# A fused beacon-attention and maxout-FFN kernel: the opening of batch 0 in another order, with fewer filler matmuls

## The chip, the cores and the metric

The kernel runs on one core of one Trainium2 chip. The metric is the device time of one execution in microseconds (us). A core has a matrix engine (TensorE, "PE" in the profile), a vector engine (VectorE, "DVE"), an activation engine (ScalarE, "ACT"), a general engine (GpSimd, "POOL") and an engine that only issues transfers (SyncE, "SP"). Each engine works through its own instructions in the order in which the program emits them, and waits at the head of its queue. Transfers between main memory (DRAM) and the on-chip memory run on sixteen shared DMA engines.

## What is computed

The reference, cut to what matters (B = 8 batches, H = 8 heads, S = 576 tokens, Nb = 16 beacons, D = 64; d_model = 512, d_ff = 768; inputs and output in float32):

```python
k_all = concatenate([beacon_k, k], axis=2)          # 16 + 576 keys
v_all = concatenate([beacon_v, v], axis=2)
scores = matmul(q, k_all.transpose(0, 1, 3, 2)) / sqrt(D)
scores = where(causal, -1e9, scores)                # beacons are seen by all
a = softmax(scores)
x = matmul(a, v_all).transpose(0, 2, 1, 3).reshape(B * S, H * D)
h = maximum(maximum(x @ w1, x @ w2), x @ w3)
out = h @ w_out                                     # 4608 x 512
```

## The kernel before, in words

**Work of attention.** Heads are taken two at a time: a *pair* is two heads of one batch, four pairs to a batch (`PPB`), 32 in all; pair p is heads 2(p mod 4) and 2(p mod 4)+1 of batch p div 4. Queries and keys of a pair arrive as rows of tokens, in bf16 or cast to it, and are turned by TensorE transposes against an identity (`turn_part` at line 331, `turn_cast` at 363, `turn_wide` at 380) or by DMA. VectorE and ScalarE copy the turned tiles from the accumulators (PSUM) into `qkT` (lines 338, 369, 387). `qkT` has room for four pairs. `turn_beacons` (line 299) and `place_beacons` (line 394) put the beacon keys ahead of the others.

Scores are computed transposed, keys by queries, in *windows* of at most 512 columns: `emit_window` gives a window's matmuls for both heads (line 476) and two exponentials on ScalarE that write the weights `at` in bf16 (line 485). `emit_mask` clears the upper triangle of a diagonal block: on GpSimd with a select (line 505), or on VectorE as a product with a 0/1 triangle `tri` (line 503). `emit_pv` multiplies weights by v with a column of ones behind it (line 529); VectorE takes the reciprocal of that column (line 539) and the product (line 541), which gives normalised rows of x. `turn_x` transposes them on TensorE (line 555) and copies them into `xT` (line 560); from batch 2 on a DMA does that.

**Work of the FFN.** The FFN is a list of *units* which `F(n)` emits in order. One unit of the first layer is a block of 128 hidden features for 512 tokens and one of the three weights (`mm1_unit`, line 592). For the first 240 tokens (`PART`), two blocks of features go together (`mm1_two`, line 606), three units for w1 and three for w2; these need only the first 240 tokens of all four pairs of batch 0. The units after them need 512 tokens. `F` emits nothing while the tokens that it needs aren't there (`avail`). VectorE drains a unit (a cast for w1 at line 582, a running maximum for w2 and w3 at line 584). Units of the second layer are `mm2_unit` (line 622), drained at line 630.

**Order of the work.** Everything is emitted in an order written out by hand. `opening()` (line 718) does batch 0 and the first window of batch 1; `loop()` (line 895) does the rest in *bursts* of three windows, and each burst emits FFN units until a goal for it is reached (`START`: 17 units by the end of burst 0, 20 by the end of burst 1).

In `opening()` the short names are: `T0(p, part)` turns part 0 (240 tokens) or 1 (336 tokens) of a pair, `W0(pi, i)` emits a window of pair pi (i = 0 is the first 240 queries; i = 2, 3, 4 are the query tiles behind them), `M0(pi, tiles, False)` masks on GpSimd and `M0(pi, tiles)` on VectorE, `P0` is the product with v, `X0` the turn of x. `idle(n)` (line 406) and `keep_busy(n)` (line 399) are matmuls of 128 and 320 columns on a tile of ones, into a bank whose content nobody reads.

**Loads of the opening.** Pairs 0 and 1 send their first part over SP and ACT as float32 (`load_part`, lines 161 and 168). The first part of pairs 2 and 3 (`load_quad(1, 0, i)`), the second part of pairs 0 and 1 (`load_quad(0, 1, i)`) and of pairs 2 and 3 (`load_quad(1, 1, i)`) are cast on the way by transfers from GpSimd's queue (line 176). So are v of batches 0 to 2 (`load_v`, line 233), the FFN weights (`load_w(i, f0, f1)` at line 282 for w1, w2, w3 as i = 0, 1, 2, each in two pieces of 512 and 256 features; `load_w_out` at line 286) and pairs 4 to 9 (`load_cast`, line 218; four buffers in turn). The beacon keys go over SP, eight small transfers (`load_beacons`, line 290). GpSimd spends time to issue each of its transfers, and its masks stand in the same queue. Later pairs come as float32 over SP (`load_wide`, line 198) and are cast by GpSimd (line 206); the first of them is held back by a memset on GpSimd. In `loop()`, `jobs` holds these loads with the burst in which each is issued.

Of the kernel before, what the change touches and what calls it, by code (L numbers as in the profile page):

```python
# [16 lines left out]
def kernel(  # L17
# [13 lines left out]
    nc = tc.nc  # L31
# [675 lines left out]
    def T0(p, part, q_copy=by_dve, k_copy=by_dve):  # L707
        turn_part(p, part, q_copy, k_copy)

    def P0(pi, *tiles):  # L710
        emit_pv(0, pi, tiles)
# [6 lines left out]
    def opening():  # L718
        keep_busy(12)
        load_part(0, 0, nc.sync)  # L720
        load_part(0, 1, nc.scalar)
        load_part(1, 0, nc.sync)
        load_part(1, 1, nc.scalar)
        load_beacons(0, 1, bk32_0)
# [15 lines left out]
        load_v(0, 0, 1)  # L740
        for i in range(2):
            load_quad(1, 1, i)
        load_w(0, 0, FA)
        cast_part(0, 0, by_dve)
        cast_part(0, 1, by_act)
        cast_part(1, 0, by_dve)
        cast_part(1, 1, by_dve)
        by_act(bk16_0, bk32_0)
        T0(0, 0, by_act)
        keep_busy(3)  # L750
        T0(1, 0)
        turn_beacons(0, 1, bk16_0)
        keep_busy(2)
        W0(0, 0)
        M0(0, (0, 1), False)
        idle(6)
        W0(1, 0)
        load_w(0, FA, d_ff)
        T0(2, 0)
        idle(6)  # L760
        T0(3, 0)
        W0(2, 0)
        idle(6)
        M0(1, (0, 1), False)
        load_v(0, 2, 3, 4)
        W0(3, 0)
        idle(6)
        M0(2, (0, 1), False)
        T0(0, 1)
        idle(6)  # L770
        W0(0, 2)
        M0(3, (0, 1))
        load_w(1, 0, FA)
        T0(1, 1)
        W0(0, 3)
        P0(0, 0, 1)
        idle(6)
        W0(0, 4)
        M0(0, (2, 3), False)
        P0(1, 0, 1)  # L780
        idle(6)
        W0(1, 2)
        load_w(1, FA, d_ff)
        X0(0, 0, 1)
        P0(2, 0, 1)
        idle(6)
        W0(1, 3)
        M0(0, (4,), False)
        T0(2, 1)
        X0(1, 0, 1)  # L790
        W0(1, 4)
        M0(1, (2, 3), False)
        P0(3, 0, 1)
        X0(2, 0, 1)
        idle(6)
        T0(3, 1)
        W0(2, 2)
        X0(3, 0, 1)
        F(1)
        load_beacons(1, B, bk32_1)  # L800
        W0(2, 3)
        M0(1, (4,), False)
        load_cast(4)
        F(1)
        W0(2, 4)
        load_cast(5)
        W0(3, 2)
        M0(2, (2, 3), False)
        F(1)
        W0(3, 3)  # L810
        M0(2, (4,), False)
        load_w(2, 0, FA)
        P0(0, 2, 3)
        P0(0, 4)
        W0(3, 4)
        load_w(2, FA, d_ff)
        M0(3, (2, 3), False)
        M0(3, (4,), False)
        X0(0, 2, 3, 4)
        P0(1, 2, 3)  # L820
        P0(1, 4)
        by_act(bk16_1, bk32_1)
        load_cast(6)
        load_v(1, 0, 1, 2, 3, 4)
        P0(2, 2, 3)
        F(1)
        X0(1, 2, 3, 4)
        turn_beacons(1, B, bk16_1)
        P0(2, 4)
        F(2)  # L830
        load_cast(7)
        turn_cast(4, by_act, by_dve)
        place_beacons(4, by_act)
        X0(2, 2, 3, 4)
        P0(3, 2, 3)
        P0(3, 4)
        emit_window(*ahead)
        X0(3, 2, 3, 4)
        F(2)
# [15 lines left out]
    jobs = []  # L855
    jobs.append((0, None, L(load_w_out, 0, n_ft // 2)))
    jobs.append((0, None, L(load_cast, 8)))
    jobs.append((0, None, L(load_v, 2, 0, 1)))
    jobs.append((1, None, L(load_w_out, n_ft // 2, n_ft)))
    jobs.append((1, None, L(load_v, 2, 2, 3, 4)))  # L860
    jobs.append((1, None, L(load_cast, 9)))
    jobs.append((1, None, L(next_load, 2)))
    for p in range(BY_CAST, NPAIR):
        if p in BY_DMA:
            jobs.append((first_burst[p] - 5, L(load_pair, p), L(cast_pair, p, by_pool)))
        else:
            gate = nc.gpsimd if p == BY_CAST else None
            c = first_burst[p] - 3
            jobs.append((c, L(load_wide, p, gate), L(cast_wide, p, by_pool)))
# [25 lines left out]
    def loop():  # L895
# [8 lines left out]
        for c, burst in enumerate(bursts):  # L904
# [10 lines left out]
            for p in range(PPB + 1, NPAIR):  # L915
                if first_burst[p] - 1 == c:
                    place_beacons(p, by_act)
                    if p < BY_CAST:
                        turn_cast(p, by_act, by_dve)
                    elif p not in BY_DMA:  # L920
                        turn_wide(p, by_act, by_dve)
# [99 lines left out]
```

## Time and profile before

| | |
|---|---|
| median of three runs | 283.21 us (283.15 to 283.51) |
| the profiled execution | 283.48 us |
| its span, first to last instruction | 281.8 us |
| TensorE busy | 275.3 us |
| GpSimd busy | 130.4 us |
| first transposes on TensorE | at 4.84 us |
| first FFN unit | at 18.65 us |
| first window of burst 1 | at 38.82 us |

Times inside the execution are counted from the start of the span. The profile names an instruction by its line in the kernel, its engine, what it writes and what it reads. A busy share says how long an engine had an instruction under way, not whether that instruction was of use; a row of the timeline gives start, length and count, and in brackets how long the engine had stood idle and what released it. The chain that ended last follows the work back from the last instruction, at each step to what released it.

### The profile page before, as it was taken

What the parts mean: (1) busy time and instruction counts of PE and PEld (TensorE: products, weight loads), DVE (VectorE), ACT (ScalarE), POOL (GpSimd) and SP (SyncE); (2) the same over time, 40 slices, a digit from 0 to 9 for tenths busy, and PEclk for the clock granted to TensorE, in tenths of its full rate; (3) what the DMA queues carried; (4) which work ended last, traced back from release to release, by engine and by line L of the source; (5) the groups of instructions that cost most, each with busy time, mean ns of one, the idle gap of its engine ahead of it and who ended that gap; (6) DMA issues with size and microseconds to landing.
All of it is one profiled execution on the core that took longest, in us unless ns stands there. A gap on an engine that the chain in (4) does not pass through costs nothing.

```text
span 281.8 us, 8016 instructions
## 1 busy us (share of the span) xinstructions
PE 275.3 (98%) x3121; PEld 158.3 (56%) x3121; DVE 198.6 (70%) x397; ACT 125.2 (44%) x274; POOL 130.4 (46%) x253
## 2 busy tenths in 40 slices
PE   7999999999999999999999999999999999999995
PEld 4678665666555555455555888555545554444442
DVE  4677776768777577667685777577757885876873
ACT  3677458887555454535553555444544100000000
POOL 8998789297664456446643645345422100000000
PEclk9999999999999999999999999999999999999999
DMA  8999999998993899999996999595342016003003
GB/s 143 187 187 197 174 131 138 238 301 194 228 190 79 264 242 217 174 295 214 237 245 182 256 221 165 157 276 134 76 130 77 0 37 198 0 0 151 0 0 150
DMA packets 87382, 45.68 MB, mean 162 GB/s; under 512 B 68400, under 2 KB 78512, under 8 KB 87344
## 3 DMA queue, kind: packets, MB, share of 16 engines
q1 hardware_dynamic: 63504, 37.25, 57.4%
q0 software_dynamic: 23488, 7.67, 25.3%
q8 instruction: 24, 0.39, 0.6%
q10 hardware_dynamic: 352, 0.25, 0.3%
q14 instruction: 14, 0.11, 0.2%
HBM read 35.13 MB, written 11.80 MB: 167 GB/s over the span
## 4 chain that ended last, share of the span: by engine, by line
PE 95%; DVE 2%; ACT 1%; issue 1%; ACTq 0%
PE ps L592 48%; PE ps L622 16%; PE ps L529 11%; PE ps L476 10%; PE ps L380 2%; PE ps L606 2%; PE ps L399 2%; PE ps L331 1%; PE ps L406 1%; PE ps L555 1%; ACT at L485 1%; PE ps L363 1%; DVE qkT L338 1%; PE ps L641 0%; DVE xT L560 0%
## 5 line engine op out<-in xcount | busy, mean ns | idle before, releaser
L592 PE MATMUL ps<-xT,w_sb 128*128 128x512 bf16 (+2 forms) x720 | 147.3, 351 | 0.1
L485 ACT ACTIVATE at<-ps 128x512 bf16<-128x512 f32 (+3 forms) x214 | 106.5, 601 | 87.8 <-PE ps L476 60.2
L592 PEld LDWEIGHTS <-w_sb 128*128 128x128 bf16 x720 | 65.4, 98 | 56.5 <-issue 4.1
L505 POOL TENSOR_SCALAR_AFFINE_SELECT at<-at 128x256 bf16<-128x256 bf16 (+2 forms) x158 | 57.3, 389 | 80.9 <-ACT at L485 71.1
L584 DVE TENSOR_TENSOR hT<-hT,ps 128x512 bf16<-128x512 bf16 (+2 forms) x111 | 74.6, 672 | 27.3 <-PE ps L592 26.2
L582 DVE CAST hT<-ps 128x512 bf16<-128x512 f32 (+2 forms) x57 | 37.7, 662 | 16.0 <-PE ps L592 13.2
L622 PE MATMUL ps<-w_out_sb,hT 128*128 128x512 bf16 x210 | 48.5, 379 | 0.0
L630 DVE COPY y<-ps 128x512 f32<-128x512 f32 x35 | 24.2, 692 | 25.2 <-PE ps L622 25.2
L529 PEld LDWEIGHTS <-at 128*128 128x128 bf16 (+1 forms) x960 | 35.5, 97 | 8.0
L529 PE MATMUL ps<-v,at 128*128 128x65 bf16 (+1 forms) x960 | 39.0, 193 | 0.0
L541 DVE TENSOR_TENSOR x<-ps,recip 128x384 bf16<-128x384 f32 (+1 forms) x68 | 32.1, 472 | 2.3
L622 PEld LDWEIGHTS <-hT 128*128 128x128 bf16 x210 | 19.6, 98 | 23.2 <-DVE hT L584 1.2
L476 PE MATMUL ps<-qkT 64*128 64x80 bf16 (+20 forms) x560 | 31.8, 243 | 0.3
L476 PEld LDWEIGHTS <-qkT 64*128 64x128 bf16 x560 | 17.9, 94 | 15.7 <-issue 10.6
L648 ACT COPY y<-ps 128x320 f32<-128x320 f32 x1 | 0.4, 425 | 56.4 <-PE ps L641 56.4
L206 POOL CAST wide<-st 128x1152 bf16<-128x1152 f32 x14 | 16.0, 1141 | 5.8 <-DMA st<-in_k_dram 5.8
L270 POOL CAST v<-st 128x512 bf16<-128x512 f32 (+2 forms) x20 | 14.0, 718 | 3.5 <-DMA st<-in_v_dram 3.5
L233 POOL DMA_DIRECT2D v<-in_v_dram x15 | 12.7, 858 | 1.1 <-DMA w_sb<-in_moe_w_dram 1.1
L539 DVE RECIPROCAL recip<-ps 128x6 f32<-128x6 f32 (+1 forms) x68 | 12.2, 179 | 0.7 <-PE ps L529 0.5
L185 POOL CAST p<-st 96x1536 bf16<-96x1536 f32 x8 | 11.7, 1460 | 0.0
L387 DVE COPY qkT<-ps 128x576 bf16<-128x576 bf16 x14 | 10.5, 749 | 0.0
L387 ACT COPY qkT<-ps 128x576 bf16<-128x576 bf16 x14 | 9.8, 701 | 0.0
(56 smaller groups left out, 116.0 us busy)
## 6 DMA issues: line engine op xcount, KB each, us to landing
out_dram<-y SPq DMA_DIRECT2D x35, 256.0 KB, 3.0
st<-in_q_dram SPq DMA_DIRECT2D x22, 288.0 KB, 6.7
st<-in_k_dram SPq DMA_DIRECT2D x22, 288.0 KB, 7.2
st<-in_v_dram SPq DMA_DIRECT2D x15, 256.0 KB, 4.7
qk_dram<-p SPq DMA_DIRECT2D x8, 288.0 KB, 4.0
w_sb<-in_moe_w_dram POOLq DMA_DIRECT2D x3, 512.0 KB, 8.1
v<-in_v_dram POOLq DMA_DIRECT2D x9, 128.0 KB, 6.1
st<-in_v_dram SPq DMA_DIRECT2D x5, 224.0 KB, 3.4
```

Source lines behind the costliest of these rows:

```text
L206: cast(t16.rearrange("p r h d -> p h r d"), st[:, 0 : 2 * WR * D].rearrange("p (h r d) -> p h r d", h=2, r=WR),)
L387: (q_copy, k_copy)[i](qkT[:, p % NT, i, Nb:NK].rearrange("d (p r) -> d p r", r=WR), pbs[i].rearrange("d (r p) -> d p r", r=WR),)
L476: nc.tensor.matmul(banks[e][:, col : col + qb - qa], qkT[hs, s, 1, 128 * t : 128 * t + 128], qkT[hs, s, 0, Nb + qa : Nb + qb], start=True, ...
L485: nc.scalar.activation(out=at[:, e, base : base + width], in_=banks[e][:, 0:width], func=AF.Exp, scale=scale,)
L505: nc.gpsimd.affine_select(out=view, in_=view, compare_op=ALU.is_ge, fill=0.0, base=x0, pattern=[[0, 2], [1, w]], channel_multiplier=-1,)
L529: nc.tensor.matmul(bank[:, c : c + GW], at[0 : k_rows[t], e, a : a + 128], v_sb[0 : k_rows[t], t, 2 * pi + e, 0:GW], start=(t == 0), stop= ...
L541: nc.vector.tensor_mul(x.rearrange("p i (e d) -> p i e d", e=2), pv[:, :, :, 0:D], recip.to_broadcast([128, n, 2, D]),)
L582: (by_act if act else by_dve)(h, bank)
L584: nc.vector.tensor_max(h, h, bank)
L592: nc.tensor.matmul(bank[:, o0 : o0 + n], w_in[i][:, ct, 128 * ft : 128 * (ft + 1)], xT[:, ct, x0 : x0 + n], start=(ct == 0), stop=(ct == n ...
L622: nc.tensor.matmul(bank, hT[:, ft, 128 * tt : 128 * (tt + 1)], w_out_sb[:, ft, :], start=(ft == 0), stop=(ft == n_ft - 1),)
L630: (by_act if act else by_dve)(y, bank)
```

## The change

Loads: in GpSimd's queue both pieces of w1 go ahead of the second part of pairs 2 and 3, and both pieces of w2 follow it at once, ahead of tiles 2 to 4 of v, which now stand behind the masks of pair 0's later windows. On SP the beacon keys of batch 0 go ahead of pair 1's queries; those of batches 1 to 7 are issued later, behind a one-column memset on VectorE. In `loop()`, pair 9's load and the first two wide loads stand further ahead, and v of batch 2 further behind.

Order: the masks of the first 240 queries are all on VectorE; the beacons are turned ahead of pair 1; `keep_busy(3)` is gone and of nine `idle(6)` there remain five `idle(5)`. The second parts of pairs 2 and 3 are turned behind the first two and three FFN units instead of ahead of the first. Pair 5 is turned in the opening instead of burst 0, which is why `loop()` starts its search one pair later. Eleven calls of units stand in the opening, eight before.

```diff
--- before.py
+++ after.py
@@ -719,9 +719,9 @@
         keep_busy(12)
         load_part(0, 0, nc.sync)
         load_part(0, 1, nc.scalar)
+        load_beacons(0, 1, bk32_0)
         load_part(1, 0, nc.sync)
         load_part(1, 1, nc.scalar)
-        load_beacons(0, 1, bk32_0)
         make_identity(nc, ident)
         for i in range(2):
             load_quad(1, 0, i)
@@ -738,105 +738,105 @@
         for i in range(2):
             load_quad(0, 1, i)
         load_v(0, 0, 1)
+        load_w(0, 0, FA)
+        load_w(0, FA, d_ff)
         for i in range(2):
             load_quad(1, 1, i)
-        load_w(0, 0, FA)
+        load_w(1, 0, FA)
+        load_w(1, FA, d_ff)
         cast_part(0, 0, by_dve)
         cast_part(0, 1, by_act)
+        by_act(bk16_0, bk32_0)
         cast_part(1, 0, by_dve)
         cast_part(1, 1, by_dve)
-        by_act(bk16_0, bk32_0)
         T0(0, 0, by_act)
-        keep_busy(3)
-        T0(1, 0)
         turn_beacons(0, 1, bk16_0)
         keep_busy(2)
+        T0(1, 0)
         W0(0, 0)
-        M0(0, (0, 1), False)
-        idle(6)
+        idle(5)
+        T0(2, 0)
         W0(1, 0)
-        load_w(0, FA, d_ff)
-        T0(2, 0)
-        idle(6)
+        idle(5)
         T0(3, 0)
+        M0(0, (0, 1))
         W0(2, 0)
-        idle(6)
-        M0(1, (0, 1), False)
-        load_v(0, 2, 3, 4)
+        idle(5)
+        M0(1, (0, 1))
+        T0(0, 1)
         W0(3, 0)
-        idle(6)
-        M0(2, (0, 1), False)
-        T0(0, 1)
-        idle(6)
+        idle(5)
+        M0(2, (0, 1))
+        T0(1, 1)
+        idle(5)
         W0(0, 2)
         M0(3, (0, 1))
-        load_w(1, 0, FA)
-        T0(1, 1)
+        P0(0, 0, 1)
         W0(0, 3)
-        P0(0, 0, 1)
-        idle(6)
-        W0(0, 4)
         M0(0, (2, 3), False)
         P0(1, 0, 1)
-        idle(6)
+        W0(0, 4)
+        M0(0, (4,), False)
+        P0(2, 0, 1)
+        X0(0, 0, 1)
         W0(1, 2)
-        load_w(1, FA, d_ff)
-        X0(0, 0, 1)
-        P0(2, 0, 1)
-        idle(6)
+        load_v(0, 2, 3, 4)
+        P0(3, 0, 1)
+        X0(1, 0, 1)
         W0(1, 3)
-        M0(0, (4,), False)
+        M0(1, (2, 3), False)
+        X0(2, 0, 1)
+        W0(1, 4)
+        M0(1, (4,), False)
+        X0(3, 0, 1)
+        load_cast(4)
+        load_cast(5)
+        nc.vector.memset(bk32_1[:, 0, 0:1], 0.0)
+        load_beacons(1, B, bk32_1)
+        F(1)
+        F(1)
         T0(2, 1)
-        X0(1, 0, 1)
-        W0(1, 4)
-        M0(1, (2, 3), False)
-        P0(3, 0, 1)
-        X0(2, 0, 1)
-        idle(6)
+        F(1)
         T0(3, 1)
         W0(2, 2)
-        X0(3, 0, 1)
-        F(1)
-        load_beacons(1, B, bk32_1)
         W0(2, 3)
-        M0(1, (4,), False)
-        load_cast(4)
         F(1)
         W0(2, 4)
-        load_cast(5)
+        load_w(2, 0, FA)
+        M0(2, (2, 3), False)
         W0(3, 2)
-        M0(2, (2, 3), False)
+        load_w(2, FA, d_ff)
         F(1)
         W0(3, 3)
+        by_act(bk16_1, bk32_1)
         M0(2, (4,), False)
-        load_w(2, 0, FA)
+        F(1)
+        W0(3, 4)
+        load_cast(6)
+        M0(3, (2, 3), False)
         P0(0, 2, 3)
         P0(0, 4)
-        W0(3, 4)
-        load_w(2, FA, d_ff)
-        M0(3, (2, 3), False)
-        M0(3, (4,), False)
-        X0(0, 2, 3, 4)
+        F(1)
         P0(1, 2, 3)
         P0(1, 4)
-        by_act(bk16_1, bk32_1)
-        load_cast(6)
+        turn_beacons(1, B, bk16_1)
+        M0(3, (4,), False)
         load_v(1, 0, 1, 2, 3, 4)
+        X0(0, 2, 3, 4)
         P0(2, 2, 3)
-        F(1)
-        X0(1, 2, 3, 4)
-        turn_beacons(1, B, bk16_1)
         P0(2, 4)
-        F(2)
-        load_cast(7)
         turn_cast(4, by_act, by_dve)
         place_beacons(4, by_act)
-        X0(2, 2, 3, 4)
+        X0(1, 2, 3, 4)
         P0(3, 2, 3)
         P0(3, 4)
+        load_cast(7)
         emit_window(*ahead)
+        X0(2, 2, 3, 4)
+        turn_cast(5, by_act, by_dve)
+        place_beacons(5, by_act)
         X0(3, 2, 3, 4)
-        F(2)
+        F(4)
 
 
 
@@ -853,13 +853,13 @@
                 last_burst[PPB * b + pi] = c
 
     jobs = []
+    jobs.append((0, None, L(load_cast, 8)))
+    jobs.append((0, None, L(load_cast, 9)))
     jobs.append((0, None, L(load_w_out, 0, n_ft // 2)))
-    jobs.append((0, None, L(load_cast, 8)))
-    jobs.append((0, None, L(load_v, 2, 0, 1)))
     jobs.append((1, None, L(load_w_out, n_ft // 2, n_ft)))
-    jobs.append((1, None, L(load_v, 2, 2, 3, 4)))
-    jobs.append((1, None, L(load_cast, 9)))
     jobs.append((1, None, L(next_load, 2)))
+    jobs.append((1, None, L(load_v, 2, 0, 1)))
+    jobs.append((2, None, L(load_v, 2, 2, 3, 4)))
     for p in range(BY_CAST, NPAIR):
         if p in BY_DMA:
             jobs.append((first_burst[p] - 5, L(load_pair, p), L(cast_pair, p, by_pool)))
@@ -912,7 +912,7 @@
                 F(max(0, k))
 
             G(2)
-            for p in range(PPB + 1, NPAIR):
+            for p in range(PPB + 2, NPAIR):
                 if first_burst[p] - 1 == c:
                     place_beacons(p, by_act)
                     if p < BY_CAST:
```

## The prediction

> **What bounds the kernel now.** I read the page first, then the busy time of the engines by stage, then the chain that ended last and the timeline of the opening.
>
> ```profile
> span 281.8 us, 8016 instructions
> PE 275.3 (98%) x3121; PEld 158.3 (56%) x3121; DVE 198.6 (70%) x397; ACT 125.2 (44%) x274; POOL 130.4 (46%) x253
> ```
>
> TensorE (PE) is busy for 98% of the span, so the time is a sum of matmuls. But the sum contains matmuls that compute nothing (lines 399 and 406), and a busy share doesn't show those. The stages are cut at 4.84 (first transposes), 18.65 (first FFN unit), 24.4 (last window of batch 0), 33.24 (burst 0) and 38.82 (first score window of burst 1).
>
> ```profile
> 4.84:18.65 13.81, 13.58 (x263) 9.59 (x263) 9.28 (x29) 9.68 (x24) 13.65 (x26) 1.00 1.69 183
> 18.65:24.40 5.75, 5.23 (x92) 3.88 (x90) 3.43 (x9) 4.54 (x11) 4.85 (x9) 1.00 1.35 201
> 24.40:33.24 8.84, 8.22 (x146) 6.66 (x147) 7.22 (x23) 3.70 (x9) 7.73 (x13) 1.00 1.56 186
> ...
> 38.82:60.00 21.18, 21.06 (x345) 12.87 (x345) 13.79 (x31) 17.77 (x40) 15.53 (x32) 1.00 1.34 204
> ```
>
> Columns: stretch, length, then busy time of PE, weight load, VectorE (DVE), ScalarE (ACT), GpSimd (POOL), granted clock, DMA share, GB/s. From 38.82 on PE idles for 0.12 us in 21. Whatever reaches that point earlier with the same useful work done keeps its gain to the end; what is changed behind it is worth nothing while PE stays full. Before it PE is also "busy", but GpSimd is busy for 13.65 of 13.81 us, DMA never rests, and VectorE has free time (4.5 us) up to 18.65. So the question is: when does burst 1's first window start? The chain gives the price of each piece of PE work, start and length:
>
> ```profile
> 5.45 0.91 PE ps L399 x3
> 7.73 0.44 PE ps L406 x6
> 14.91 0.27 PE ps L476 x6
> 16.24 0.42 PE ps L331 x12
> 20.21 0.33 PE ps L476 x8
> 20.54 0.93 PE ps L606 x8
> 23.18 0.84 PE ps L529 x24
> 33.31 0.56 PE ps L476 x10
> 35.53 3.35 PE ps L592 x28
> ```
>
> **The change: what it takes away.** Of nine `idle(6)` five `idle(5)` stay: 29 matmuls fewer at 0.44/6 = 0.073 us, 2.1 us. `keep_busy(3)` goes: 0.91 us. If nothing waited in their place, that would be 3.0 us. The rest of this part asks what waits in their place, in three steps.
>
> **Step 1, to the first FFN unit.** The first beacon load is issued one place sooner on SP (by one issue, 0.43 us).
>
> ```profile
> 1.74 4.55 SPq L290 DMA_DIRECT2D bk<-in_beacon_k_dram  x8
> 5.52 0.62 ACT L748 CAST bk<-bk 16x512 bf16<-16x512 f32 x1 [0.95 <-DMA bk<-in_beacon_k_dram]
> 7.39 0.33 PE L476 MATMUL ps<-qkT 64*128 64x240 bf16 x4
> ```
>
> Its cast then runs from 5.1 to 5.7, the beacon transposes at 5.8, the two fillers and the transposes of pair 1 follow, and the first score window comes at 7.1 instead of 7.39. The query load that now stands behind it on SP lands 0.43 us later, at 5.1; its cast is over by 5.9, before PE asks for it at 6.5. From 7.1 PE needs two windows, two fillers and one transpose group (0.27, 0.37, 0.34, 0.26, 0.37) until the transposes of pair 3 start at 8.7; their first copy can start at 9.05. From there VectorE has a full queue, as the six masks of pairs 0 to 2 now stand on it as well. Its spacing, read from starts that follow each other (a duration overlaps the next by about 0.08):
>
> ```profile
> 8.70 1.57 DVE L338 COPY qkT<-ps 128x240 bf16<-128x240 bf16 x4 [1.24 <-PE ps L331]
> ...
> 12.26 0.47 DVE L503 TENSOR_TENSOR at<-at,tri 128x224 bf16<-128x224 bf16 x2
> ...
> 12.94 0.92 DVE L338 COPY qkT<-ps 128x336 bf16<-128x336 bf16 x2 [0.21 <-PE ps L331]
> ...
> 26.31 0.17 DVE L539 RECIPROCAL recip<-ps 128x2 f32<-128x2 f32 x1
> ...
> 26.72 0.17 DVE L539 RECIPROCAL recip<-ps 128x4 f32<-128x4 f32 x1
> ...
> 27.27 0.65 DVE L584 TENSOR_TENSOR hT<-hT,ps 128x480 bf16<-128x480 bf16 x1
> ...
> 29.94 0.75 DVE L369 COPY qkT<-ps 128x576 bf16<-128x576 bf16 x1
> ...
> 30.61 0.32 DVE L560 COPY xT<-ps 128x336 bf16<-128x336 bf16 x1
> 30.85 0.17 DVE L539 RECIPROCAL recip<-ps 128x4 f32<-128x4 f32 x1
> ```
>
> A small copy takes 0.37, a mask 0.20, a copy pair of a second part 0.84, the pair reciprocal and product 0.55 (two tiles) or 0.41 (one), a copy of x 0.24, a copy of a whole pair 0.67. Pair 3's copies 0.74, eight masks 1.6, the second parts of pairs 0 and 1 1.68, four products 2.2, four copies of x 0.96: 7.2 us, so the last copy of x starts near 16.0 and the first FFN unit, which waits for it, goes on at 16.25 and ends at 16.8. In the trace it was:
>
> ```profile
> 19.54 0.67 PE L606 MATMUL ps<-xT,w_sb 128*128 128x240 bf16 x5 [0.43 <-DVE xT L560]
> ...
> 20.58 4.66 ACT L485 ACTIVATE at<-ps 128x512 bf16<-128x512 f32 x10 [1.08 <-PE ps L476]
> ...
> 26.05 0.98 PE L606 MATMUL ps<-xT,w_sb 128*128 128x240 bf16 x8
> ```
>
> It ended at 20.15 (the other two rows serve below), but 1.12 us of work (two transpose groups, one window) was then done that now stands behind it. So much of the deleted filler turns into waits for VectorE: by 16.8 about 2.2 us are won.
>
> **Step 2, to the last window of batch 0.** PE has five units (4.6), two transpose groups (0.84) and six windows (1.8) to do, 7.2 us: until 24.05, with all six units of the first 240 tokens done (the seventh `F(1)` issues nothing, as it needs 512 tokens). Here the loads decide. Pair 2 and 3's second part now stands behind 768 KB of weights in GpSimd's queue, and the two loads of w2 (`load_w(1, ...)`) ahead of 336 KB of v.
>
> ```profile
> q0 software_dynamic: 8709, 2.63, 122.5%
> q1 hardware_dynamic: 1504, 0.51, 13.2%
> ...
> w_sb<-in_moe_w_dram POOLq DMA_DIRECT2D x2, 512.0 KB, 8.1
> w_sb<-in_moe_w_dram POOLq DMA_DIRECT2D x2, 256.0 KB, 8.0
> v<-in_v_dram POOLq DMA_DIRECT2D x3, 128.0 KB, 7.4
> ...
> bk<-in_beacon_k_dram SPq DMA_DIRECT2D x8, 32.0 KB, 4.2
> ```
>
> ```profile
> L282 POOL DMA_DIRECT2D w_sb<-in_moe_w_dram x1: 806/806/806, 14.7 to 14.7; - x1
> DMA to landing us min/median/max: 8.1/8.1/8.1
> ```
>
> The first fence is the first 20 us: GpSimd's queue moved 2.63 MB. The second: the first half of w2 was issued at 14.7 and landed at 22.8, when the 2.85 MB up to it had passed (six query and key loads, v of batch 0, w1, itself). Now v's last three tiles stand behind it and 2.51 MB are enough; 0.34 MB at about 0.2 MB per us (the last column by stage) are 1.7 us, so 21.1. The seven later beacon loads, about half of q1's 13.2% (1.2 to 1.5 us of the engines), leave the first 10 us too, but come back behind a memset on VectorE near 16.4 and meet the weights; I credit half a us. PE asks for w2 at 20.1. The price is between nothing (19.4) and 2.7 us (22.8, no relief); I take 0.5 us, nearest to the interpolated row. By the same count the second part of pairs 2 and 3 lands at about 17.9, for 17.75: inside that 0.5, as the same queue holds both. Tiles 2 to 4 of v land 0.6 MB behind w2's half, at 23.6 to 24.5, and are asked for from 24.5 on: bounds 0 and 1.0, I take 0.3.
>
> SP holds nothing behind the gated beacon loads until burst 2. On ScalarE their cast now stands ahead of the last window's exponentials: the loads land at 16.4 + 7 x 0.43 + 4.2 = 23.6, and the cast's turn comes behind ten exponentials (4.66) from 19.9 on, at 24.5: nothing. Behind it wait two exponentials, a mask and the last product of pair 3, which has about 0.8 us to spare.
>
> **Step 3, to burst 1.** VectorE is the bound again: four pairs of products (0.96 each), four copies of x (0.24), two whole-pair copies (0.67, that of pair 5 now included): 6.1 us from 24.7 (0.6 us into the first products' matmuls), so 30.9. `F(4)` waits for the last one and then takes 1.6 us more (four units at 3.35/7, less three matmuls begun before); the window of burst 0 0.56 and seven units 3.35 end at 36.4 without the waits on DMA, at 37.2 with them. Before:
>
> ```profile
> 38.82 0.84 PE L476 MATMUL ps<-qkT 64*128 64x48 bf16 x16
> ```
>
> The units left for burst 0 are seven, as 17 is its goal: nothing is left undone. **Sum: 38.8 - 37.2 = 1.6 us.** The rest of the change is priced at nothing: pair 9's two loads stand ahead of w_out and v of batch 2, whose users come in burst 3 or later; the two wide loads are freed about 4 us sooner, on GpSimd, which PE doesn't wait for there (0.12 us idle in 21). If that cover failed, the price would be the wait itself. GpSimd loses six masks and gains none.
>
> The profiled execution took 283.48, 1.7 us outside its span; less 1.6 is 281.9. The median of the three runs is 283.21, so 281.6.
>
> **Rivals.**
>
> *The weights come too late (slower).* Without waits on DMA for w2 the gain is 2.1 us. PE is in order: if w2's first half lands at L, the fourth unit holds all behind it for L - 20.1. At L = 22.2 nothing is gained; from 22.8 it is slower by over 0.2%. 22.8 is exactly its landing today, and then the time is 283.8; with the seven beacon loads in its way (1.2 us) 285.0. For it: the DMA share is over 1.3 from 4.84 to 33.24, and the demand moves by 6 us (26.05 to 20.1) where the landing moves by 2. Against: 0.34 MB really do leave its way. Chance 0.20.
>
> *VectorE takes all.* Counted at their full durations, steps 1 and 3 are 2 us longer, which leaves nothing: 283.2. For it: both steps hang on its queue, and it takes over six masks. Against: the starts above are measured. Chance 0.12.
>
> *The clock stays low longer.* The first matmuls of the filler run slower than the last ones (shortest, median, longest in ns):
>
> ```profile
> L399 PE MATMUL ps<-busy x17: 299/474/474, 1.5 to 7.2; 128*128 128x320 bf16 x17
> ```
>
> The quick ones are the last, near 7.1. If the three deleted fillers are what speeds PE up there, the speed-up comes later. By this row the windows, fillers and transposes of the next 3 us are up to 1.6 times longer; some 2 us of work there would cost 1.0 to 1.5 us, and a part is hidden under VectorE: gain 0.6, so 282.6. The granted clock shows 1.00 in every stage, the first too, so it doesn't settle it. Chance 0.10, half on either side of 0.2%.
>
> The Trainium skill (TensorE: Matmul & The Clock Gate, Part 1) says that the clock doubles only after a free-running window of about 3.4 us in which PE was busy enough, and Part 4 that transposes don't count as busy in the same way. By that rule the change, which leaves PE waiting from 5.4 to 5.8 and fewer fillers than before between 3.7 and 7.1, could lose the window. The rows of 474 and 299 ns agree with a doubling; no run here shows the threshold yet.
>
> **How the numbers follow.** Forecast, 280.5 to 282.6: 0.58. With half of the clock's case, faster by over 0.2% (0.57 us, about what a measurement can tell) 0.63; within 0.17 (VectorE, half of the clock); slower 0.20. The range goes from 280.4 (no wait on DMA and a little more) to 284.2 (w2 near 23.2), leaving out about 0.2.
>
> **What would show it.** Right: 25 matmuls on line 406; eight masks on line 503; the first unit going on near 16.3 after a wait for VectorE's copy of x; burst 1's first window near 37.2; w2's first half landing at 20 to 21; the rest of the trace shifted as a block. Wrong: PE waiting at its fourth or first unit for a weight load; matmuls of 128x320 and 64x240 still slow after 7.1; a wait for ScalarE behind the beacons' cast; a new wait behind 38.

## The result and the profile after

The changed kernel takes 290.86 us (median of four runs, 289.94 to 291.41); the kernel before, run beside it, 283.36. The ratio is 1.0247, with a 95% interval of 1.0208 to 1.0287. The forecast was 281.6: the sign was wrong, and the time lies above the range. Most executions of the kernel before take 283.0 to 283.8 us, but 17 of its 92 in the four groups below take 284.65 to 286.06, so medians are compared.

The profiled execution took 290.44. The head of its page, beside the one of before:

```profile
span 288.7 us, 7943 instructions
PE 276.2 (96%) x3089; PEld 157.9 (55%) x3089; DVE 198.9 (69%) x404; ACT 125.4 (43%) x274; POOL 128.7 (45%) x247
...
PEclk9999999996899999999999999999999999999999
```

Fewer matmuls (3089 for 3121) have a slightly longer busy time, 12.5 us of the span are idle where 6.5 were, and the granted clock has a dip in the tenth and eleventh slice (65 to 79 us). Next, the stages up to 80 us, cut at the first window of burst 1, first of before and then of after (columns as in the prediction):

```profile
1.53:38.82 37.29, 35.92 (x581) 25.96 (x581) 25.60 (x74) 21.68 (x49) 33.44 (x59) 1.00 1.51 176
...
60.00:80.00 20.00, 20.00 (x292) 11.51 (x289) 15.18 (x35) 14.10 (x34) 13.85 (x27) 1.00 1.01 228
```

```profile
1.53:38.91 37.38, 34.04 (x548) 24.44 (x549) 25.69 (x81) 21.81 (x49) 29.85 (x51) 1.00 1.49 174
38.91:60.00 21.09, 20.97 (x342) 12.78 (x342) 13.76 (x30) 17.67 (x39) 17.54 (x35) 1.00 1.36 182
60.00:80.00 20.00, 15.93 (x208) 9.04 (x206) 10.27 (x24) 10.24 (x25) 9.32 (x18) 0.83 1.09 245
```

Two things are to be read here. **The opening is a draw**: TensorE is busy 1.9 us less, but idles 3.34 us for 1.37, and burst 1 starts at 38.91, for 38.82. **The loss is behind it**: from burst 1's first window to the end of the span after takes 249.8 us (288.7 less 38.9) and before 243.0, so 6.8 of the 6.9 us. In the 20 us from 60 on TensorE does 208 matmuls for 292. The timeline of TensorE there shows why:

```profile
63.98 0.41 PE L529 MATMUL ps<-v,at 128*128 128x65 bf16 x8
64.99 0.37 PE L529 MATMUL ps<-v,at 128*128 128x65 bf16 x7 [0.60 <-DMA v<-in_v_dram]
68.83 0.98 PE L529 MATMUL ps<-v,at 128*128 128x65 bf16 x15 [3.47 <-DMA v<-in_v_dram]
69.75 1.46 PE L476 MATMUL ps<-qkT 64*128 64x272 bf16 x16
71.14 3.39 PE L592 MATMUL ps<-xT,w_sb 128*128 128x512 bf16 x8
```

The first products of batch 2 wait twice for v, 4.07 us in all. And the FFN unit pair behind them, eight matmuls of 512 columns, takes 3.39 us; the same eight take 1.90 elsewhere. Stretches of one and two us show the granted clock, the third column from the right:

```profile
66.00:67.00 1.00, 0.00 (x0) 0.00 (x0) 0.16 (x1) 0.00 (x0) 0.70 (x1) 1.00 1.00 276
67.00:68.00 1.00, 0.00 (x0) 0.00 (x0) 0.00 (x0) 0.00 (x0) 0.00 (x0) 0.69 1.27 280
...
72.00:74.00 2.00, 2.00 (x6) 0.72 (x5) 0.69 (x1) 1.57 (x5) 1.43 (x6) 0.50 0.88 241
74.00:76.00 2.00, 2.00 (x36) 1.09 (x35) 1.43 (x3) 0.64 (x1) 2.00 (x3) 0.95 1.32 196
```

A mean of 0.69 puts the fall to 0.5 at 67.4, in the middle of the wait; a mean of 0.95 puts its end at 74.2. From 68.8 on TensorE works at half speed for 5.4 us, which loses up to 2.7 us. The waits of 4.07 and these 2.7 are the 6.8.

Why is v late? Its loads in GpSimd's queue, the first and last of six wide transfers on SP (L198: the two wide loads that the change moves, and the next one, with two transfers each), and the time from issue to landing of v, of after:

```profile
44.59 1.72 POOL L233 DMA_DIRECT2D v<-in_v_dram  x2
47.64 2.50 POOL L233 DMA_DIRECT2D v<-in_v_dram  x3
```

```profile
44.14 0.73 SPq L198 DMA_DIRECT2D st<-in_q_dram  x1
...
48.23 0.62 SPq L198 DMA_DIRECT2D st<-in_k_dram  x1
```

```profile
DMA to landing us min/median/max: 9.5/16.5/20.3
```

and of before:

```profile
39.17 1.73 POOL L233 DMA_DIRECT2D v<-in_v_dram  x2
43.87 2.53 POOL L233 DMA_DIRECT2D v<-in_v_dram  x3
```

```profile
47.80 0.72 SPq L198 DMA_DIRECT2D st<-in_q_dram  x1
...
51.16 1.40 SPq L198 DMA_DIRECT2D st<-in_k_dram  x1
```

```profile
DMA to landing us min/median/max: 5.0/5.4/5.9
```

Before, v is issued first and lands in 5 to 6 us. After, six transfers of 288 KB are ahead of it or beside it, and v lands 15 to 20 us after its issue (the 9.5 is the small load of beacon values). At 5 to 6 us it would have been there 9 us ahead of its use at 64; the lateness of the issue alone costs nothing.

### The profile page after: what moved, and what is told of

It is laid out like the page before. It is cut to its first block, busy times and chain, and to the rows that moved or that the text cites. A ratio compares the mean times of both kernels' runs of the same rounds, so it can differ in the third digit from the quotient of the medians.

```text
span 288.7 us, 7943 instructions
## 1 busy us (share of the span) xinstructions
PE 276.2 (96%) x3089; PEld 157.9 (55%) x3089; DVE 198.9 (69%) x404; ACT 125.4 (43%) x274; POOL 128.7 (45%) x247
## 4 chain that ended last, share of the span: by engine, by line
PE 77%; DMA 11%; POOL 8%; issue 1%; DVE 1%; ACT 0%; POOLq 0%; ACTq 0%
PE ps L592 45%; PE ps L622 14%; PE ps L529 9%; DMA v<-in_v_dram 7%; PE ps L476 7%; DMA w_sb<-in_moe_w_dram 4%; POOL at L505 2%; PE ps L380 2%; POOL quad L176 1%; POOL w_sb L282 1%; POOL v L233 1%; POOL p L218 1%; POOL w_out_sb L286 1%; PE ps L363 1%; PE ps L641 0%
## 5 line engine op out<-in xcount | busy, mean ns | idle before, releaser
L505 POOL TENSOR_SCALAR_AFFINE_SELECT at<-at 128x256 bf16<-128x256 bf16 (+2 forms) x152 | 55.1, 388 | 84.7 <-ACT at L485 77.0
L529 PE MATMUL ps<-v,at 128*128 128x65 bf16 (+1 forms) x960 | 39.8, 194 | 4.5 <-DMA v<-in_v_dram 4.1
```

Of the source, the lines that this page charges most:

```text
L505: nc.gpsimd.affine_select(out=view, in_=view, compare_op=ALU.is_ge, fill=0.0, base=x0, pattern=[[0, 2], [1, w]], channel_multiplier=-1,)
L529: nc.tensor.matmul(bank[:, c : c + GW], at[0 : k_rows[t], e, a : a + 128], v_sb[0 : k_rows[t], t, 2 * pi + e, 0:GW], start=(t == 0), stop= ...
```

## The experiments

Theory A: the loss is v of batch 2 behind the early wide loads. Rival B: v is issued too late. Theory C, on the missing gain: the new first 7 us let TensorE wait before its clock has risen, and it stays at half speed. Rival D: the deleted matmuls stood beside other waits and are worth nothing. The kernel before measured 283.35, 283.31, 283.34 and 283.20 us in the four groups of runs (experiments 1 to 4, 5 to 8, 9 to 12, 13 to 15). For each profiled execution I give "burst 1", the start of its first window, and "the rest", the span less that; before has 38.82 and 243.0, after 38.91 and 249.8.

### The loop's loads

**Experiment 1: after, with the job list of before.**

```diff
-    jobs.append((0, None, L(load_cast, 8)))
-    jobs.append((0, None, L(load_cast, 9)))
     jobs.append((0, None, L(load_w_out, 0, n_ft // 2)))
+    jobs.append((0, None, L(load_cast, 8)))
+    jobs.append((0, None, L(load_v, 2, 0, 1)))
     jobs.append((1, None, L(load_w_out, n_ft // 2, n_ft)))
+    jobs.append((1, None, L(load_v, 2, 2, 3, 4)))
+    jobs.append((1, None, L(load_cast, 9)))
     jobs.append((1, None, L(next_load, 2)))
-    jobs.append((1, None, L(load_v, 2, 0, 1)))
-    jobs.append((2, None, L(load_v, 2, 2, 3, 4)))
```

> The changed kernel with the order of loads in the loop (w_out, pairs 8 and 9, v of batch 2, first wide loads) as before the change; the new opening stays. Theory (the whole loss comes from the new order of these loads: v of batch 2 lands 18 to 20 us after its issue and TensorE waits 4.1 us for it, then runs at half clock): 283.4 us, within 0.4 of the kernel before, as burst 1 starts at 38.91 in the changed kernel against 38.82; no wait for v behind 60 us. Rival (the new opening leaves a backlog in GpSimd's transfer queue, and v of batch 2 is late because of it): 287 us or more, with a wait for v of over 2 us still there.

283.84 us (282.01 to 285.67; ratio 1.001, 0.9975 to 1.0046). No wait for v; burst 1 at 39.80, rest 243.2. The whole loss behind burst 1 is the job list. Burst 1 is later than in after, with the same opening; the clock fell there:

```profile
6.00:9.00 3.00, 2.25 (x42) 1.62 (x42) 2.24 (x7) 1.18 (x3) 3.00 (x5) 0.92 1.64 163
9.00:12.00 3.00, 3.00 (x41) 1.80 (x40) 2.23 (x9) 1.35 (x4) 2.75 (x4) 0.50 1.51 145
...
15.00:18.00 3.00, 2.83 (x62) 1.88 (x60) 2.62 (x10) 2.88 (x8) 1.41 (x4) 0.94 1.40 189
```

Half clock from about 8.5 to 15.4. Seven of the ten executions have a mean clock of 0.985 to 0.988, as this one; of the two at 1.000 one is the fastest, 282.01, the other 283.9.

**Experiment 2: before, with the job list of after.**

> The kernel before with only the new order of loads in the loop. Theory (that order alone): 290 us, with a wait of some 4 us for v of batch 2 near 65 us and a lower clock behind it. Rival (the opening's backlog): within 0.5 of the kernel before, 283.4.

285.31 us (283.84 to 291.65; ratio 1.0049, 1.0013 to 1.0085), widely scattered. The profiled execution was the longest of the ten (291.65): it waits 3.95 us for v, burst 1 at 40.23, rest 249.7. So in this execution the list alone costs nearly 7 us behind burst 1, but on the median it costs 2.0, and neither theory (290) nor rival (283.4) has that. No profile of a shorter execution was kept, so why they lose less isn't shown; experiment 11 bears on it.

**Experiment 3: after, the wide loads behind v, v as late as in after.**

```diff
-    jobs.append((1, None, L(next_load, 2)))
     jobs.append((1, None, L(load_v, 2, 0, 1)))
     jobs.append((2, None, L(load_v, 2, 2, 3, 4)))
+    jobs.append((2, None, L(next_load, 2)))
```

> The changed kernel with the first two wide loads behind all of v of batch 2 instead of ahead of it; v stays as late as in the change. Theory in the form 'the wide loads on SP, 1.7 MB issued at 44 to 49, take the transfer engines from v': v lands about 6 us after its issue, no wait, 283.5 to 284. In the form 'v is issued too late' (last tile at 50 instead of 46): wait and time hardly change, 289 to 291. A new wait of GpSimd's cast for the wide loads, as in the kernel before, may cost up to 1.

284.59 us (283.3 to 286.0; ratio 1.0022, 0.9981 to 1.0064). Burst 1 is at 39.88, behind a dip of the clock in the opening as in experiment 1; the rest is 243.0, with no wait for v, although it is issued as late as in after:

```profile
45.51 1.72 POOL L233 DMA_DIRECT2D v<-in_v_dram  x2
48.55 2.51 POOL L233 DMA_DIRECT2D v<-in_v_dram  x3
51.19 0.72 SPq L198 DMA_DIRECT2D st<-in_q_dram  x1
```

```profile
DMA to landing us min/median/max: 5.7/6.4/6.8
```

A stands, B falls: the same late loads land in 6 us when the wide ones are behind them.

**Experiment 4: after, all of v one burst sooner, still behind the wide loads.**

```diff
-    jobs.append((2, None, L(load_v, 2, 2, 3, 4)))
+    jobs.append((1, None, L(load_v, 2, 2, 3, 4)))
```

> The changed kernel with tiles 2 to 4 of v of batch 2 issued in burst 1 again, still behind the wide loads. 'The wide loads take the engines from v': tiles 2 to 4 are some 1 to 2 us sooner, the wait shrinks from 4.1 to 2 or 3 us, 288 to 289.5. 'v is issued too late': no wait, 283.5.

288.9 us (285.9 to 292.28; ratio 1.015, 1.0063 to 1.0236). Wait for v 4.1 us, landing 9 to 21 us after issue, rest 249.0. So v issued sooner, but still behind the wide loads, is waited for as long as in after (2 to 3 us were expected): the other half of the same answer.

**Experiment 5: after, with matmuls without use where the wait was.**

```diff
                 b, pi = divmod(p, PPB)
+                if p == 2 * PPB:
+                    idle(60)
                 emit_pv(b, pi, (0, 1, 2))
```

> The changed kernel with 60 filler matmuls (4.4 us at 0.073) ahead of the first product of batch 2, where TensorE waits for v. Theory (the loss of 7 us is the wait of 4.1 and, for the rest, half a clock for some 6 us behind it): TensorE stays at full clock, the wait is filled and not lengthened, so 2.5 to 3 us less than the changed kernel: 287.5 to 288.5. Rival (the rest comes from the late loads themselves, not from the clock): no less than the changed kernel, 290 to 291.

288.97 us (286.86 to 289.75; ratio 1.0179, 1.0128 to 1.0231): 1.9 below after, where theory asked for 2.5 to 3 and the rival for none. The clock stays at 1.00 from 65 to 75, there is no wait for v, and the rest is 247.7, 4.7 above before and 2.1 below after. What the 4.7 are:

```profile
55.84 2.10 PE L622 MATMUL ps<-w_out_sb,hT 128*128 128x512 bf16 x9 [1.18 <-DMA w_out_sb<-in_moe_w_out_dram]
...
66.64 3.51 PE L406 MATMUL ps<-busy 128*128 128x128 bf16 x60
```

The fillers hold the next matmul up for 3.35 us (66.64 to 69.99), not for the 4.4 that were planned, and a wait of 1.18 us for w_out stands ahead of them that after doesn't have: 4.5 of the 4.7. So a TensorE that is kept busy here doesn't lose its clock, and nothing is left over for half speed. Of the 6.8 us of after, 4.07 are the wait, read from its timeline, and the 2.7 that remain are what 5.4 us at half speed lose.

**Experiment 11: after, with the first 7 us of before** (its order of loads, casts and fillers up to the first window, and idle(6)).

```diff
-        load_beacons(0, 1, bk32_0)
         load_part(1, 0, nc.sync)
         load_part(1, 1, nc.scalar)
+        load_beacons(0, 1, bk32_0)
...
-        by_act(bk16_0, bk32_0)
         cast_part(1, 0, by_dve)
         cast_part(1, 1, by_dve)
+        by_act(bk16_0, bk32_0)
         T0(0, 0, by_act)
+        keep_busy(3)
+        T0(1, 0)
         turn_beacons(0, 1, bk16_0)
         keep_busy(2)
-        T0(1, 0)
```

> The changed kernel with only the first 7 us of before (as the ninth kernel), and with its own job list. Theory (loss = late v of batch 2 plus the half clock that follows; the opening's gain is there once the start is the old one): a wait of 3 to 4 us for v at the third batch's first products, 5 to 7 us more than the ninth kernel, 287.5 to 289.5. Rival (the long loss depends on the slow start): under 4 us more than the ninth.

285.15 us (284.38 to 285.8; ratio 1.0065, 1.0042 to 1.0087): the rival was right, 1.4 us above experiment 9. Burst 1 is at 39.30 and the rest 244.5. The second half of w_out is late first (a wait of 0.92 us at line 622), and v then lands 11.5 to 17.1 us after issue, with 0.18 us to wait. (In this profile the first half of w2, too, is waited for 1.89 us, up to 22.67.) In the profiles of after and of experiments 2 and 4, w_out lands sooner (median 8.3, 8.2 and 7.8 us), nobody waits for it, and the last of v takes 20.3, 19.8 and 21.1 us; in those of 5 and 11 w_out takes 9.4 and 9.2 and v 17.3 and 17.1. It looks like a race in which a small delay of TensorE is worth several us.

**Experiment 15: after, held for about a microsecond before burst 3.**

```diff
+            if c == 3:
+                idle(14)
             for w in burst:
```

> The changed kernel with 14 small matmuls without use (1.0 us) ahead of burst 3's windows, when v of batch 2 and the wide loads are already issued. Theory (a race: TensorE's products wait for the late v, and a microsecond of delay lets the output stores and the next two wide loads, which stand behind TensorE's results, go later, so that v lands sooner): wait for v under 2 us, clock kept, 285 to 288. Rival (v lands late whatever TensorE does; its lateness comes with the new start): the filler only replaces part of the wait, 290 to 292.

286.42 us (285.55 to 289.2; ratio 1.0131, 1.0094 to 1.0168): 0.9 us of useless work (14 fillers, from 48.47 to 49.34) takes 4.4 us off. The wait for v:

```profile
67.61 0.62 PE L529 MATMUL ps<-v,at 128*128 128x65 bf16 x15 [0.93 <-DMA v<-in_v_dram]
```

```profile
DMA to landing us min/median/max: 9.9/14.7/17.8
```

That a short delay of TensorE lets v land sooner is shown: v lands up to 17.8 us after issue instead of 20.3, TensorE asks later, the clock doesn't fall behind the gap of 0.93 us, and the rest is 244.8. Burst 1 is at 40.21 here, but that isn't the reason: it is at 40.23 in experiment 2's profile, which has no such delay and waits 3.95 us. That it is the next output stores and wide loads on SP, issued behind TensorE's results, which go out of v's way is my reading of the timelines and wasn't tried by itself.

### The first 7 us

**Experiments 7 and 8: experiment 1 with the order of SP's loads of before and five fillers at one place; 8 also reads w1 where w2 is used for the first 240 tokens** (that part of the FFN is left out).

```diff
-        keep_busy(2)
+        keep_busy(5)
         T0(1, 0)
```

> The run with the old order of loads in the loop, and ahead of pair 1 the old five warm-up matmuls and the old order on SP (pair 1's queries ahead of the beacons). Theory (the new opening alone gains 1.3 us at full clock, and lost it in most executions to half a clock from 8.4 to 15.2): clock 1.0 in nearly all executions, 281.8 to 282.4. Rival (the transfers hold the opening, whatever the clock): 283.2 to 283.8.

> As the run before, but the units of the first 240 tokens that should use w2 use w1, so TensorE doesn't wait for w2 there (w2 is left out for these tokens, the work is the same). Theory (the wait for w2 was 0.8 us and passes on to burst 1): 0.5 to 1.0 us less than the run before. Rival (v tiles 2 and 3, next in the same queue, are waited for instead): no more than 0.3 less.

285.5 us (282.25 to 286.52; ratio 1.0051, 1.0012 to 1.009) and 285.42 (282.72 to 286.68; 1.0045, 1.0011 to 1.008). As many fillers as before did not help: two executions of the seventh kernel take 282.25, the other eight over 285.2. These two and the 282.01 of experiment 1 are the nearest that the whole computation with the new opening comes to the forecast; no profile of them was kept. The profiled ones are slow from the start to about 16.8 us, with burst 1 at 40.54 and 41.13 and rests of 243.2 and 243.0; that hid w2's price in the eighth, which settles nothing. The granted clock shows 1.00 there all the same; only the durations tell it. The 128-column filler of the seventh kernel and of before, from 7 to 15 us:

```profile
L406 PE MATMUL ps<-busy 128*128 128x128 bf16 x21 | 3.1, 307 | 0.0
```

```profile
L406 PE MATMUL ps<-busy 128*128 128x128 bf16 x42 | 3.5, 220 | 0.0
```

The fillers stand behind the beacons, and TensorE waits ahead of them for the beacons' cast, 0.55 us at 5.45.

**Experiment 12: before, with only the first 7 us of after.**

> The kernel before with only the new first 7 us: beacons ahead of pair 1 on SyncE, their cast first, three fillers fewer, the transposes of pair 1 behind the beacons; all else as before. Theory (the new start loses the speed-up): slow spells in the profile between 5 and 17 us in most executions, first window of burst 1 no sooner or later than 38.82, time 283.3 to 286, scattered. Rival (the fillers were free): 282.3 to 282.8, closely grouped.

285.61 us (285.49 to 285.7; ratio 1.0082, 1.0067 to 1.0097). All four executions lose 2.3 us. Burst 1 at 41.03, rest 243.0, and from 7 to 15 us

```profile
L406 PE MATMUL ps<-busy 128*128 128x128 bf16 x30 | 4.0, 303 | 0.0
```

for 220 ns before. That the new first 7 us cost these 2.3 us is shown: the only edits are the beacons ahead of pair 1, three fillers fewer and pair 1 last. Which of them does it isn't. TensorE idles here from about 6.3 to 6.6 for pair 1's query:

```profile
6.64 0.68 PE L331 MATMUL ps<-ident,h 80*64 80x80 bf16 x12 [0.34 <-DVE h L168]
```

This fits theory C: its two fillers just ahead, at 5.58, are still slow. But it doesn't prove it. Experiment 2's profile, with the old first 7 us and no idle spell in them, is slow to about 10.6 us, and after's own, with the new ones and 0.44 us idle, is at full speed from 5.9.

**Experiment 9: experiment 1 with the first 7 us of before** (the diff of experiment 11).

> The changed kernel with the loop's job list of before and with the first 7 us of before: the loads of pair 1 ahead of the beacons, three fillers between the transposes of pair 0 and pair 1, and idle(6) in place of idle(5). Theory (the new start lets TensorE wait at 5.4 to 6.6 us, before it has sped up, and so in most executions it stays or falls back to half speed for some 7 us): full speed again in nearly every execution, first window of burst 1 near 38.0, time 282.0 to 282.6, closely grouped. Rival (the slow spells come from the loads or from the dense first 20 us, not from the first waits): slow spells as often as in the first experiment, 283.5 to 285 on the median.

283.71 us (282.74 to 287.46; ratio 1.0007, 0.9983 to 1.0031). The clock is at 0.998 or more in nine of ten executions and eight take 282.7 to 284.1, so the long openings are rarer, as C expects. But burst 1 is at 38.96, not at 38.0, rest 242.9. So full speed alone doesn't bring the gain. The waits of its TensorE up to 38 us:

```profile
6.52 0.25 PE L299 MATMUL ps<-ident,bk 16*128 16x16 bf16 x4 [0.37 <-ACT bk L751]
10.46 0.34 PE L331 MATMUL ps<-ident,quad 112*64 112x112 bf16 x6 [0.26 <-DMA quad<-in_k_dram]
15.37 0.38 PE L476 MATMUL ps<-qkT 64*128 64x128 bf16 x7 [0.18 <-ACT at L485]
21.53 0.99 PE L606 MATMUL ps<-xT,w_sb 128*128 128x240 bf16 x8 [0.74 <-DMA w_sb<-in_moe_w_dram]
26.36 1.07 PE L529 MATMUL ps<-v,at 80*128 80x65 bf16 x30 [0.21 <-DMA v<-in_v_dram]
28.27 0.37 PE L299 MATMUL ps<-ident,bk 112*128 112x112 bf16 x4 [0.83 <-ACT bk L812]
33.45 1.67 PE L592 MATMUL ps<-xT,w_sb 128*128 128x272 bf16 x13 [0.36 <-DVE xT L560]
```

2.95 us, where before shows 0.69 in two waits. 24 short fillers fewer, at about 0.06 us (experiment 5 has 60 in 3.51), are 1.4 us: all of it turned into waits, for six different releasers.

**Experiment 10: experiment 9, with w1 read where w2 is used for the first 240 tokens** (that part of the FFN is left out).

```diff
-                    w_in[i][:, ct, 128 * (ft + f) : 128 * (ft + f + 1)],
+                    w_in[0][:, ct, 128 * (ft + f) : 128 * (ft + f + 1)],
```

> As the ninth kernel, but every matmul of the first FFN's units of the first 240 tokens and after reads the first weight in both halves, so TensorE never waits for the second weight there (that part of the FFN is left out; instructions and loads stay as many). Theory (the second weight lands after TensorE asks for it, 0.5 to 0.8 us): 0.4 to 0.9 us less than the ninth kernel. Rival (the wait only moves to the next load, v's last tiles, or to VectorE): within 0.3 us of the ninth.

282.86 us (282.19 to 286.07; ratio 0.9984, 0.9944 to 1.0023). 0.85 us below experiment 9 on the medians, burst 1 0.70 sooner at 38.26: that is the price of w2's landing. Part of the wait moved on: TensorE waits 1.1 us for v here, 0.21 in experiment 9. The intervals of 9 and 10 overlap; the two profiles carry the reading.

### Fewer fillers in the old order

**Experiment 6: before without keep_busy(3), and with five idle(5) for nine idle(6).**

> The kernel before with the three warm-up matmuls of keep_busy(3) out and five idle(5) in place of nine idle(6), nothing else. Theory of the prediction (filler on the path): up to 3.0 us less; with waits for VectorE in its place 1 to 2 less: 281 to 282.5. Rival (fewer matmuls let the clock fall): a stretch of some 6 us at a granted clock of 0.5 between 8 and 16 us in most executions, mean clock near 0.986, and 283.5 to 285.

283.49 us (282.72 to 285.3; ratio 0.9994, 0.9962 to 1.0025). The theory's 281 to 282.5 is missed. Burst 1 at 38.07, 0.75 sooner, rest 243.9: given back behind the opening, at

```profile
55.30 0.70 PE L363 MATMUL ps<-ident,p 96*64 96x96 bf16 x24 [0.85 <-DMA p<-in_k_dram]
```

Pair 9 is the next load that comes late. The change's moving it forward has its reason here.

**Experiments 13 and 14: before with five idle(5), or idle(2), for nine idle(6), keep_busy(3) kept, and pair 9's load right behind pair 8's.**

```diff
     jobs.append((0, None, L(load_cast, 8)))
+    jobs.append((0, None, L(load_cast, 9)))
...
-    jobs.append((1, None, L(load_cast, 9)))
```

> The kernel before with five idle(5) in place of nine idle(6), keep_busy(3) and the order of the opening kept, and pair 9's two loads right behind pair 8's in burst 0; v of batch 2 and the wide loads as before. Theory (with full clock and pair 9 in time, what the opening gains is kept to the end; the sixth experiment gained 0.75 us up to burst 1 and lost 0.85 to pair 9): first window of burst 1 at 38.0 to 38.4, no wait for pair 9, 282.5 to 282.9. Rival (deleted filler only turns into waits, or another load is late next): within 0.3 us of before.

> As the thirteenth kernel with five idle(2): 15 small matmuls fewer, 1.1 us. Theory (they stand beside VectorE's masks and copies, which set the pace there, and hold the clock up): 0 to 0.4 us less than the thirteenth kernel, or slow spells after 7 us. Rival (they are on the path): 0.8 to 1.1 us less.

283.21 us (282.71 to 285.5; ratio 0.9996, 0.997 to 1.0022) and 282.8 (282.65 to 285.03; 1.0000, 0.9976 to 1.0024). The thirteenth comes out as its rival said, the fourteenth 0.4 below it. Burst 1 at 38.10 and 37.99: 15 fillers fewer bring 0.11 us, so those stood beside waits, as rival D says. Pair 9 is no longer waited for. The thirteenth's profile loses 1.1 us at the next place, a wait of line 622 for VectorE at 58.33; the fourteenth's has no wait behind burst 1, its rest is 243.0, and it took 282.67. Its median is 0.4 us below before, and six of its eleven executions are at or under 282.8, where the fastest of 23 of before is 282.97; but the interval of its ratio holds 1, so this is the best version tried, and not one shown to be faster.

## Why the prediction was wrong

**The step that failed** is in step 3: "The rest of the change is priced at nothing: pair 9's two loads stand ahead of w_out and v of batch 2, whose users come in burst 3 or later; the two wide loads are freed about 4 us sooner, on GpSimd, which PE doesn't wait for there (0.12 us idle in 21)." The users do come late, at 64 us. But that the two wide loads, with the next one behind them, are six transfers of 288 KB on SP, and that v of batch 2 now has to land behind and beside them, was not worked out: the step counted issue places and not landings. The cover was some 9 us at the landing time of before (5.4 us) and less than none at the new one (17 to 20 for the last three tiles). Experiment 3 takes only this away, and with it all 6.8 us. "If that cover failed, the price would be the wait itself" was too small as well: 4.07 us were the wait, and 2.7 the half clock that follows it, which stays away when TensorE is kept busy (experiment 5).

How the wide loads hold v up can be read from the packets of the two queues in after:

| from, to (us) | SP's queue | GpSimd's queue (v) |
|---|---|---|
| 50 to 56, wide loads under way | 623 packets, 1.28 MB | 697 packets, 0.09 MB |
| 56 to 60, SP's queue nearly empty | 145 packets, 0.28 MB | 3345 packets, 0.42 MB |
| 62 to 69, output stores and later loads | 2400 packets, 1.91 MB | 172 packets, 0.02 MB |

Beside the wide loads v gets about as many packets as they do, but its packets hold some 130 bytes and theirs 2 KB; most of v moves in the four microseconds in which SP's queue is nearly empty, and the little that is left at 62 takes 7 us more. The Trainium skill (DMA: Bandwidth & Descriptors, Queues, rings and completion order) says that a DMA engine goes round the queues that have work, one packet at a time. The first row agrees with it, if what the profile counts as packets are the same packets. No run here varied the size of a packet.

The loss behind burst 1 isn't all that was missed: with the old list the new opening takes 283.84 us (experiment 1), not 281.6. The gain of 1.6 us was missing too, and steps 1 to 3 show where.

**Step 1** was right in its result. Two units were done at 17.9 (the row of the timeline: start 15.79, 2.10 us for 16 matmuls), so the first, which takes half, at about 16.8, as forecast. It was wrong in a part: the cast of pair 1's query, forecast to be over by 5.9 and unneeded until 6.5, kept TensorE waiting from 6.18 to 6.62. A filler is also cheaper than the 0.073 us of the sum: at 0.06 the 29 deleted ones are 1.7 us, not 2.1.

```profile
6.62 0.57 PE L331 MATMUL ps<-ident,h 80*64 80x80 bf16 x12 [0.44 <-DVE h L168]
...
15.79 2.10 PE L606 MATMUL ps<-xT,w_sb 128*128 128x240 bf16 x16
...
18.49 0.34 PE L331 MATMUL ps<-ident,quad 112*64 112x112 bf16 x6 [0.34 <-DMA quad<-in_k_dram]
21.43 0.99 PE L606 MATMUL ps<-xT,w_sb 128*128 128x240 bf16 x8 [0.76 <-DMA w_sb<-in_moe_w_dram]
26.19 1.38 PE L529 MATMUL ps<-v,at 128*128 128x65 bf16 x39 [0.46 <-POOL at L505]
30.60 0.39 PE L476 MATMUL ps<-qkT 64*128 64x512 bf16 x2 [0.32 <-DVE qkT L369]
32.27 0.45 PE L363 MATMUL ps<-ident,p 96*64 96x96 bf16 x12 [0.65 <-issue]
38.91 0.84 PE L476 MATMUL ps<-qkT 64*128 64x48 bf16 x16
```

**Step 2** had the right mechanisms and sizes somewhat too small: w2 and the second parts were put at 0.5 us and v's last tiles at 0.3, 0.8 in all; these rows show 0.76, 0.34 and 0.46, 1.56 in all (the third is ended by v's tile 3, issued at 16.06 and landing 10.1 us later, although the mask is named). The pair of experiments 9 and 10 prices w2 alone at 0.7 to 0.85. w2's first half landed at 21.4, forecast 20.6 to 21.1.

**Step 3** had two waits that were not forecast, 0.32 and 0.65 us before 33. With the 0.76 us by which step 2 was too small they make 1.73, and 1.71 lie between 37.2, the forecast for burst 1, and 38.91. The profile names no releaser for the wait of 0.65.

**The clock's rival** had the right place and too small a price: 1.0 to 1.5 us of loss, part of it hidden, with a chance of 0.10. Experiment 12 measures 2.3 us, in four of four executions, on the old opening. It isn't what made the profiled execution of after long, since that one is at full speed from 5.9 us on. The prediction's sentence on the Trainium skill (TensorE: Matmul & The Clock Gate, Part 1), by which the clock rises only after a free-running window that was busy enough, agrees with how much the rise varies here: with the same first 7 us it comes at 5.9 in after and not before 14 us in experiment 12. That the number of fillers is not the whole point is suggested by experiments 6 (three fewer, no idling but 0.25 us: at full speed by 7 us in its profile) and 7 (as many, but behind an idle 0.55 us: slow to 16.8). That the idle spell is the cause stays open, as experiment 12 says.

**The rival on the other side** (w2 too late) had the sign, not the cause: its price is 0.76 us in after (1.89 in the profile of experiment 11), against the 6.8 behind burst 1.

## What to carry to other kernels

When a load is moved, work out its landing and not its issue: list what every queue has under way from then to its first use, and take the landing time from a row where it had such company. A wait of several us on TensorE costs itself and the half clock behind it. And when matmuls without use are deleted, first compare the durations of the first matmuls, as the granted clock may not show a slow start, and then ask which load is late next.

## What the runs showed of the hardware

- The clock fell 2.0 us into the 3.47 us wait (at 67.4; idle since 65.36, and for 0.60 us of the microsecond before) and came back 6.8 us later. In experiment 1 the dip lasts 6.8 us too (8.5 to 15.4), with TensorE busy nearly all the time: it comes 1.9 us after the end of an idle spell of only 0.73. In experiment 11 a wait of 1.89 us up to 22.67 brought no fall.
- At the start of an execution TensorE can run at half speed to 16.8 us while the granted clock says 1.00 (307 ns for 220 per 128-column filler, experiment 7).
- The same loads of v of batch 2, 16 to 128 KB, land after 5.0 to 5.9 us ahead of six transfers of 288 KB, and after up to 21.1 behind and beside them.
- Two queues with work got about as many packets each, 623 and 697 in 6 us, and so 1.28 and 0.09 MB (after, 50 to 56 us).
- A delay of 0.9 us on TensorE can bring 4.4 us (experiment 15).
